# Adding epsilon by a reduction over (row sum, epsilon) pairs, with a newly set order of the work, in a fused attention and feed-forward kernel

## The chip, the cores and the metric

One core of one Trainium2 chip runs the whole program. The metric is device microseconds (us) of one execution of that core; lower is better. All data is float32.

## The reference

Block-causal attention over 8 batches of 8 heads (576 tokens, head width 64, blocks of 64), then two matrix products with a leaky ReLU between them on the 4608 x 512 result:

```python
scores = scale * np.matmul(q, k.transpose(0, 1, 3, 2))
scores = np.where(block_i >= block_j, scores, -1000000000.0)
scores = scores - np.max(scores, axis=-1, keepdims=True)
attn = np.exp(scores)
attn = attn / (np.sum(attn, axis=-1, keepdims=True) + 1e-09)
x = np.matmul(attn, v)            # heads side by side: 4608 x 512
h = x @ w_in                      # 512 x 2048
out = np.maximum(0.01 * h, h) @ w_out   # 2048 x 512
```

## The kernel before

Attention works head by head. The 576 query rows of a head are five tiles of up to 128 rows, tile t having 64, 192, 320, 448 or 576 keys. A head of the later batches goes through two softmax groups: tiles 3 and 2 (two rows of statistics, "128x2"), then tiles 4, 1 and 0 ("128x3"). The first batch is handled as 16 half heads. For each group `softmax` (line 502) plans: the score products on PE (TensorE) into the one PSUM pair `p_s` (L485 and L495); a mask and a negated row maximum `nm` on DVE (VectorE; L510 and L517); the exponential on ACT (ScalarE, L526), which also accumulates the row sums `sums`; then the pair of DVE instructions that the change is about, `sums + EPS` into `rec` (L541) and the reciprocal in place (L542); then `normalising` (line 548), which multiplies each row of probabilities `prow` by `rec` on POOL (GpSimd, L555), DVE (L556) or ACT (L557).

From the third batch on, the normalised rows are transposed in 32 x 32 pieces by DVE (`turn`, L733) and brought into place by a round trip through DRAM (`way`, `ptm`; L750 and L757, issued by SP). Every operand of a product is split into a high and a low float32r part: the high part is a cast (L244 on ACT, L245 on DVE), the low part a subtraction (L254 on DVE, L255 on POOL). So there are `pt` (probabilities), `vs`, `ks`, `qs` (L468), `xh`/`xl` (the feed-forward input) and `gh`/`gl` (the activated hidden layer).

The feed-forward layer takes the attention result in 18 chunks of 256 tokens. Each chunk has eight steps; a step is 24 products into `p_h` (L835), the activation `g` on ACT (L842), its split into `gh` and `gl`, and 12 products into `p_o` (L854). It runs behind the attention, and the two are interleaved on PE.

The order on every engine is set by a planner. Each piece of work is added with a rank, a cost in ns and the engines that could do it; `Plan.run` (line 104) walks through a time of its own and issues, on each free engine, the ready piece of lowest rank. The costs written in the program, the ranks' offsets (the table `RL` to `FILLTO`, lines 37 to 58) and the engine choices thus decide the order, which is then fixed in the program; on the chip every engine works through its list in order. A `DVE+` cost marks work that the planner doesn't put beside POOL work; L541 and L542 are marked plain `DVE` with 275 ns for both.

```python
def reciprocals():
    nc.vector.tensor_scalar_add(rec[z][:, a:e], sums[z][:, a:e], EPS)
    nc.vector.reciprocal(rec[z][:, a:e], rec[z][:, a:e])

add([("DVE", 275, reciprocals)], r, [("sum", z, at_col[t]) for t in ts], ...)
```

Of the kernel before, what the change touches and what calls it, by code (L numbers as in the profile page):

```python
# [9 lines left out]
F32 = mybir.dt.float32  # L10
# [3 lines left out]
ALU = mybir.AluOpType  # L14
AX = mybir.AxisListType
PSUM = bass.MemoryType.PSUM

P = 128
# [3 lines left out]
NT = 5  # L22
NEG = -1000000000.0
EPS = 1e-9
# [9 lines left out]
RAWS = 3  # L34
VALS = 3

RL = 1.277
RP = -34.119
RB = -28.274
RT = 2.311  # L40
RV = 3.081
RX = -25.651
RN = -61.868
RM = 0.934
RC = 15.092

LEAD = 2.356
LAG = 1.993
RS = 2.117
RG = 8.192  # L50
OFF1 = 4.961
SL1 = 10.108
AHEAD = -1.863

LAT = 1550
HOLD = 79.261
FILL = 235
FILLTO = -31.779


LOAD = 109
# [4 lines left out]
class Plan:  # L66
# [19 lines left out]
    def add(self, choices, rank, reads=(), writes=(), lag=0, kind=None):  # L86
        i = len(self.ops)
        deps = set()
        for k in reads:
            if k in self.writer:  # L90
                deps.add(self.writer[k])
        for k in writes:
            if k in self.writer:
                deps.add(self.writer[k])
            deps.update(self.readers.get(k, ()))
        for k in reads:
            self.readers.setdefault(k, []).append(i)
        for k in writes:
            self.writer[k] = i
            self.readers[k] = []  # L100
        deps.discard(i)
        self.ops.append((choices, rank, deps, lag, kind))

    def run(self):
# [15 lines left out]
        def offer(i):  # L120
            for k, choice in enumerate(self.ops[i][0]):
                e = choice[0]
                e = e[:3] if e == "DVE+" else e
                at = max([0] + [ends[d][1] + self.SYNC.get((ends[d][0], e), 0) for d in self.ops[i][2]])
                heapq.heappush(waiting, (at + k * HOLD, i, k))

# [101 lines left out]
def attention_ffn(ctx: ExitStack, tc: tile.TileContext, qk: bass.AP, v: bass.AP, w_in: bass.AP, w_out: bass.AP, out: bass.AP):  # L228
    nc = tc.nc
# [10 lines left out]
    add = plan.add  # L240
# [25 lines left out]
    def fixed(shape, dt, name, n=None, pool=const):  # L266
        if n is None:
            return pool.tile(shape, dt, name=name)
        return [pool.tile(shape, dt, name=f"{name}{i}") for i in range(n)]
# [20 lines left out]
    qn = [64, 128, 128, 128, 128]  # L290
# [13 lines left out]
    ks = fixed([P, 2, S], F32R, "ks", 2)  # L304
    kh, kl = ([ks[z][:, y] for z in range(2)] for y in range(2))
    vs = fixed([P, NT, 2 * D], F32R, "vs")
    nm = fixed([P, NT], F32, "nm", 2)
    sums = fixed([P, NT], F32, "sums", 2)
    rec = fixed([P, NT], F32, "rec", 2)
    for y in range(2):  # L310
        nc.gpsimd.memset(sums[y], 1.0)
    xr = [fixed([P, ND, S], F32, "xr0"), None]
    p_s = fixed([P, 2, 512], F32, "p_s", pool=psum)
    p_t = fixed([P, 512], F32, "p_t", 2, pool=psum)
# [40 lines left out]
    def weight_piece(num, rank, f, out_side, c0):  # L355
# [28 lines left out]
        if src.dtype != F32:  # L384
# [3 lines left out]

            add([("SP", 475, load)], rank - AHEAD, [], [r_key, t_key], lag=dma(w * P * 8))
            add(copying(w, val, top, by=2.0**-112), rank, [t_key], [v_key])  # L390
# [16 lines left out]
        else:  # L407
# [3 lines left out]

            add([("SP", 475, load)], rank - AHEAD, [], [v_key], lag=dma(w * P * 4))
        add(copying(w, lambda: hi, lambda: shaped(val())), rank, [v_key], [(key, 0)])
        add(subtracting(w, lambda: lo, lambda: shaped(val()), lambda: hi, "POOL"), rank, [v_key, (key, 0)], [(key, 1)])

    def attention(i):
        n, kind = work[i]
        b, h = divmod(n, H)
        z = i % 2
        r0 = float(i)  # L420
        y = z if b == 1 else 0
# [29 lines left out]

        add([("SP", {"full": 475, "lo": 650, "hi": 1300}[kind], load)], r0 - RL, [], [qkey], lag=dma((qe - qa + ke) * rows * 4))
        if plain_v:
            vt, vkey = lambda: vf[z][:, :nv], ("vf", z)
        else:
            vt, vkey = lambda: later["v_stage"][:, :nv], "vt"
        add([("SP", 475, lambda: nc.sync.dma_start(vt(), v[b, h, :, :nv]))], r0 - RL + 0.1, [], [vkey], lag=dma(nv * P * D * 4))
        rp = r0 - RP
        q_in, k_in = lambda: qkt()[:rows, 0, qa:qe], lambda: qkt()[:rows, 1, :ke]
# [40 lines left out]
        at_col = [(t - 2) % NT if kind == "full" else t for t in range(NT)]  # L500

        def softmax(tiles, mms, masks, r, both=None):
            banks = sorted({(sk, bk) for _, _, bk in tiles for bk in bk})
            add([("PE", list(scores(mms)))], r, qkd, banks)
            if both is not None:
                add([merging(*both, BLK)], r, [], banks)

            def mask():
                for ap in masks:
                    nc.vector.memset(ap, NEG)  # L510

            if masks:
                add([("DVE", sum(82 if len(ap.shape) == 2 else 140 for ap in masks), mask)], r, [], banks)
            for t, ap, bk in tiles:
                flat = len(ap.shape) == 2
                add(
                    [("DVE", dve(kw[t]), lambda t=t, ap=ap, flat=flat: nc.vector.tensor_reduce(  # L517
                        nm[z][: qn[t], at_col[t] : at_col[t] + 1], ap[: qn[t]], axis=AX.X if flat else AX.XY, op=ALU.max, negate=True
                    ))], r, [(sk, x) for x in bk], [("nm", z, at_col[t])],
                )  # L520

            def exponent(t, ap, flat):
                o = row(t, qn[t], pc[t], kw[t])
                if not flat:
                    o = o.rearrange("p (a k) -> p a k", a=2)
                nc.scalar.activation(  # L526
                    o, ap[: qn[t]], AF.Exp, bias=nm[z][: qn[t], at_col[t] : at_col[t] + 1], scale=1.0,
                    accum_out=sums[z][: qn[t], at_col[t] : at_col[t] + 1],
                )

            for t, ap, bk in tiles:
                add(
                    [("ACT", act(kw[t]) + 190, lambda t=t, ap=ap: exponent(t, ap, len(ap.shape) == 2))], r,
                    [("nm", z, at_col[tt]) for tt, _, _ in tiles] + [(sk, x) for x in bk], pkeys(t) + [("sum", z, at_col[t])],
                )

            ts = [t for t, _, _ in tiles]
            a, e = min(at_col[t] for t in ts), max(at_col[t] for t in ts) + 1

            def reciprocals():  # L540
                nc.vector.tensor_scalar_add(rec[z][:, a:e], sums[z][:, a:e], EPS)  # L541
                nc.vector.reciprocal(rec[z][:, a:e], rec[z][:, a:e])  # L542

            add([("DVE", 275, reciprocals)], r, [("sum", z, at_col[t]) for t in ts], [("rec", z, y) for y in range(a, e)])
            for t, _, _ in tiles:
                add(normalising(t, qn[t]), r - RN, [("rec", z, at_col[t])], pkeys(t))

# [24 lines left out]
        if kind != "lo":  # L572
# [3 lines left out]
            if kind == "full":  # L576
# [5 lines left out]
                masks = [pair(p_s[:BLK, 1, 224:480], 3)]  # L582
            softmax(tiles, mms, masks, r0 + RB, both)
        if flip:
            turn(i, row, pkeys)
        for base, c0, w, items in () if flip else tgroups[kind]:
            x = bank()
# [4 lines left out]

            add([("PE", [transpose(*y) for y in items])], r0 + RT, [k for t in sorted({a for a, _, _ in items}) for k in pkeys(t)] + ["ident"], [("t", x)])
            src = p_t[x][:, c0 : c0 + w]
            if plain_v:
                hi = ptf[:, base : base + w]
                add(copying(w, lambda hi=hi: hi, lambda src=src: src, sb=False), r0 + RT, [("t", x)], [("ptf", base)])
                continue
# [4 lines left out]
            def lo(base=base, w=w):  # L603
                return later["pt"][:, 1, base : base + w]

            add(copying(w, hi, lambda src=src: src, sb=False), r0 + RT, [("t", x)], [("pth", base)])
            add(
                subtracting(w, lo, lambda src=src: src, hi, sb=False)[:1],
                r0 + RT, [("t", x), ("pth", base)], [("ptl", base)],
            )  # L610
# [4 lines left out]
        vkey = ("vf", z) if plain_v else "vs"  # L615
        rv, rx = r0 + RV, r0 + RX

# [103 lines left out]
    def turn(i, row, pkeys):  # L721
# [6 lines left out]
        def flipped(t, s0, s1, step, j, r=0, n=P, k=1):  # L728
# [5 lines left out]

            add([("DVE", dve(k * P), go)], r0 + RT, pkeys(t), [("turn", t, j)])

# [11 lines left out]
        for b in range(4):  # L748
            add(
                [("SP", 475, lambda b=b: nc.sync.dma_start(way[z][b], later["turn"][:, b * w : (b + 1) * w]))],  # L750
                r0 + RM, ready, [("way", z, b)], lag=dma(P * w * 4),
            )
        for b in range(4):
# [4 lines left out]

            add([("SP", 475, back)], r0 + RM, [("way", z, b)], [("ptm", b)], lag=dma(P * w * 4))
        got = [("ptm", b) for b in range(4)]  # L760
        for a in range(4):
            hi = lambda a=a: later["pt"][:, 0, a * w : (a + 1) * w]
            lo = lambda a=a: later["pt"][:, 1, a * w : (a + 1) * w]
            raw = lambda a=a: later["ptm"][:, a * w : (a + 1) * w]
            add(copying(w, hi, raw), r0 + RC, got, [("pth", bases[a])])
            add(subtracting(w, lo, raw, hi), r0 + RC, got + [("pth", bases[a])], [("ptl", bases[a])])

# [56 lines left out]
    def ffn1(c, u, rank):  # L824
# [3 lines left out]
        for i in range(2):  # L828
# [11 lines left out]
            add([("PE", steps)], rank + i / 1000, ks + wkeys[("wi", f)], [("h", z)])  # L840
        rank += RG
        add([("ACT", act(512), lambda: nc.scalar.activation(g, hh, AF.Prelu, alpha=0.01))], rank, [("h", z)], ["g"])  # L842
# [33 lines left out]
    for num, (f, o, c) in enumerate(pieces):  # L876
        kind = "wo" if o else "wi"
        wkeys.setdefault((kind, f), []).extend([((kind, f, c), 0), ((kind, f, c), 1)])
        weight_piece(num, OFF1 + SL1 * (num + 1) / len(pieces), f, o, c)
    ready = []  # L880
# [5 lines left out]
    for i in range(len(work) + 1):  # L886
# [4 lines left out]
        if i in events:  # L891
# [3 lines left out]
            for k in range(num):  # L895
                c, u = here[k // NU], k % NU
                rank = i + LEAD + (nxt - i) * k / num
                if u == 0:
                    split_x(c, rank - RS)
                ffn1(c, u, rank)  # L900
# [41 lines left out]
```

## Time and profile before

| | us |
|---|---|
| median of 3 runs (1139.65 to 1141.52) | 1139.75 |
| the profiled execution | 1139.62 |
| its span, first to last instruction | 1137.9 |
| PE busy | 1082.0 (95%) |
| DVE busy | 856.8 (75%) |
| ACT busy | 686.9 (60%) |
| POOL busy | 484.0 (43%) |
| mean granted TensorE clock | 0.992 |

The program has stages with different limits: up to about 250 us the weights are loaded and split while the first batch is attended to; from 250 to about 970 us attention and feed-forward run side by side, less densely from 500 to 650 us; after that only the feed-forward layer is left. The shares of busy time over the whole span mix these stages, so the views are read by stretches. Busy PE time is a modelled figure, since products overlap.

### The profile page before, as it was taken

The page shows a single profiled execution, that of the slowest core. Times are in us where ns is not written, and L with a number is a line of the kernel's source. Part 1 is how long each engine was busy: PE and PEld are TensorE (multiplying, and loading weights), DVE is VectorE, ACT ScalarE, POOL GpSimd, SP SyncE. Part 2 cuts the span into 40 slices and gives each one's busy share as a digit, 9 for nine tenths or more (in the row PEclk, how much of TensorE's full clock was granted, in tenths as well). Part 3 has the DMA queues.
Part 4 walks back from the last instruction along what each step waited for, and adds up shares of the span by engine and source line. Part 5 has one row for each costly group of instructions (what it writes and reads, how often), then busy time and mean ns, then how long its engine had stood idle before and what let it go on. Part 6 is the DMA issues. An engine that isn't in the chain of part 4 may idle for free.

```text
span 1137.9 us, 20109 instructions
## 1 busy us (share of the span) xinstructions
PE 1082.0 (95%) x6792; PEld 961.0 (84%) x6792; DVE 856.8 (75%) x2047; ACT 686.9 (60%) x1637; POOL 484.0 (43%) x422
## 2 busy tenths in 40 slices
PE   6799999889998999899999999989999999999998
PEld 4577899778897988799999898879888898999997
DVE  6989888889899999967667699998999998400000
ACT  6888776768666666655555566666666766422222
POOL 2323454445544555433434445454544454322221
PEclk9999999989999999999999999999999999999999
DMA  6776331267665656454554565656666654300000
GB/s 201 226 215 219 115 102 54 86 185 227 202 180 161 197 163 188 150 166 128 157 153 129 164 182 164 186 163 176 177 199 175 180 164 147 84 19 10 11 19 19
DMA packets 94246, 166.20 MB, mean 146 GB/s; under 512 B 9664, under 2 KB 79296, under 8 KB 94144
## 3 DMA queue, kind: packets, MB, share of 16 engines
q1 hardware_dynamic: 94144, 164.93, 49.4%
q8 instruction: 53, 0.87, 0.4%
q14 instruction: 49, 0.40, 0.1%
HBM read 111.41 MB, written 53.48 MB: 145 GB/s over the span
## 4 chain that ended last, share of the span: by engine, by line
PE 53%; DVE 20%; ACT 8%; issue 7%; DMA 7%; POOL 3%; SPq 1%; DVEq 0%; POOLq 0%; ACTq 0%
PE p_h L835 22%; PE p_o L854 20%; PE p_s L495 4%; ACT prow L526 4%; DVE nm L517 4%; PE p_t L670 3%; DMA v_stage<-in_v 3%; DVE turn L733 2%; DVE rec L541 2%; DVE xl L254 2%; POOL gl L255 2%; DVE pt L254 2%; PE p_t L591 2%; POOL vs L255 1%; DMA out<-ob 1%
## 5 line engine op out<-in xcount | busy, mean ns | idle before, releaser
L835 PE MATMUL p_h<-xl,wih 128*128 128x256 f32 x1152 | 323.5, 281 | 9.1 <-DVE xl L254 9.1
L255 POOL TENSOR_TENSOR gl<-g,gh 128x512 fp32r<-128x512 f32 x131 | 177.0, 1351 | 355.4 <-ACT gh L244 218.7
L835 PE MATMUL p_h<-xh,wih 128*128 128x256 f32 x1152 | 326.1, 283 | 0.5 <-ACT xh L244 0.5
L835 PE MATMUL p_h<-xh,wil 128*128 128x256 f32 x1152 | 322.0, 279 | 0.0
L835 PEld LDWEIGHTS p_h<-xl,wih 128*128 128x128 f32 x1152 | 219.2, 190 | 21.1 <-DVE xl L254 11.6
L835 PEld LDWEIGHTS p_h<-xh,wih 128*128 128x128 f32 x1152 | 218.6, 190 | 10.3 <-ACT xh L244 0.7
L526 ACT ACTIVATE prow<-p_s,nm 128x576 f32<-128x576 f32 (+4 forms) x308 | 159.8, 526 | 101.4 <-DVE nm L517 100.6
L835 PEld LDWEIGHTS p_h<-xh,wil 128*128 128x128 f32 x1152 | 218.8, 190 | 0.0
L854 PE MATMUL p_o<-woh,gh 128*128 128x512 f32 x576 | 182.2, 398 | 0.0
L854 PE MATMUL p_o<-wol,gh 128*128 128x512 f32 x576 | 179.8, 394 | 0.0
L854 PE MATMUL p_o<-woh,gl 128*128 128x512 f32 x576 | 179.4, 393 | 0.0
L842 ACT ACTIVATE g<-p_h 128x512 f32<-128x512 f32 x144 | 85.1, 591 | 150.4 <-PE p_h L835 143.6
L255 POOL TENSOR_TENSOR pt<-ptm,pt 128x448 fp32r<-128x448 f32 x120 | 144.0, 1215 | 51.2 <-DVE pt L245 24.3
L557 ACT ACTIVATE prow<-prow,rec 128x320 f32<-128x320 f32 (+4 forms) x227 | 121.9, 571 | 71.6 <-DVE rec L542 68.7
L733 DVE STREAM_TRANSPOSE turn<-prow 128x384 f32<-128x384 f32 (+3 forms) x384 | 140.9, 397 | 18.5 <-ACT prow L557 6.2
L517 DVE TENSOR_REDUCE nm<-p_s 128x1 f32<-128x576 f32 (+4 forms) x308 | 137.8, 479 | 2.6
L854 PEld LDWEIGHTS p_o<-woh,gl 128*128 128x128 f32 x576 | 108.5, 188 | 24.1
L854 PEld LDWEIGHTS p_o<-wol,gh 128*128 128x128 f32 x576 | 108.9, 189 | 23.6
L495 PE MATMUL p_s<-ks,qs 128*128 128x288 f32 (+4 forms) x616 | 110.8, 314 | 19.0 <-ACT prow L526 18.4
L495 PEld LDWEIGHTS p_s<-ks,qs 128*128 128x128 f32 x616 | 89.5, 192 | 29.4 <-ACT prow L526 27.3
L670 PE MATMUL p_t<-pt,vs 128*128 128x512 f32 (+2 forms) x464 | 101.3, 348 | 1.1 <-DVE pt L254 1.0
L541 DVE TENSOR_SCALAR rec<-sums 128x3 f32<-128x3 f32 (+2 forms) x136 | 82.4, 606 | 24.5 <-ACT prow L526 19.9
(84 smaller groups left out, 1466.4 us busy)
## 6 DMA issues: line engine op xcount, KB each, us to landing
way<-turn SPq DMA_DIRECT2D x192, 224.0 KB, 2.3
ptm<-way SPq DMA_DIRECT2D x192, 224.0 KB, 4.3
qk_in<-in_qk SPq DMA_DIRECT2D x56, 576.0 KB, 4.8
v_stage<-in_v SPq DMA_DIRECT2D x56, 160.0 KB, 2.4
out<-ob SPq DMA_DIRECT2D x35, 256.0 KB, 2.4
raw<-in_w_in SPq DMA_DIRECT2D x16, 512.0 KB, 4.5
raw<-in_w_out SPq DMA_DIRECT2D x16, 512.0 KB, 4.3
qk_in<-in_qk SPq DMA_DIRECT2D x8, 320.0 KB, 3.7
```

What stands on the lines that cost most here:

```text
L254: ("DVE+" if sb else "DVE", dve(n), lambda: nc.vector.tensor_sub(dst(), one(), two())),
L255: ("POOL", pool2(n), lambda: nc.gpsimd.tensor_sub(dst(), one(), two())),
L495: go = lambda ap=ap, cols=cols, moving=moving, first=first, last=last: nc.tensor.matmul(ap, qs[z][:, cols], moving, start=first, stop=last)
L517: [("DVE", dve(kw[t]), lambda t=t, ap=ap, flat=flat: nc.vector.tensor_reduce(nm[z][: qn[t], at_col[t] : at_col[t] + 1], ap[: qn[t]], axis= ...
L526: nc.scalar.activation(o, ap[: qn[t]], AF.Exp, bias=nm[z][: qn[t], at_col[t] : at_col[t] + 1], scale=1.0, accum_out=sums[z][: qn[t], at_co ...
L541: nc.vector.tensor_scalar_add(rec[z][:, a:e], sums[z][:, a:e], EPS)
L557: ("ACT", act(kw[t], True), lambda: nc.scalar.mul(p(), p(), by)),
L670: nc.tensor.matmul(to, vs[:, j, :], src, start=start, stop=stop)
L733: nc.vector.transpose(dst, src.rearrange("p (s b i) -> p s b i", b=4, i=32))
L835: nc.tensor.matmul(hh[:, i, :], w[:, d, f * P : (f + 1) * P], x[:, d, :], start=k == 0, stop=k == len(terms) - 1)
L842: add([("ACT", act(512), lambda: nc.scalar.activation(g, hh, AF.Prelu, alpha=0.01))], rank, [("h", z)], ["g"])
L854: nc.tensor.matmul(p_o[m], a[:, i, m * P : (m + 1) * P], w[:, 2 * u + i, :], start=u == 0 and k == 0, stop=u == NU - 1 and k == 5,)
```

## The change

The row sums get a second column that holds epsilon, written once at the start by POOL. The scalar addition becomes a reduction over each (sum, epsilon) pair, on the same engine and in the same place before the reciprocal. The tiles of `nm` and `rec` become slices of one tile. The planner's cost of the pair goes from 275 to 290 ns, and 20 of its ordering constants get new values, of which two are shown.

```diff
-RG = 8.192
+RG = -1.11
...
-HOLD = 79.261
+HOLD = 64.646
...
-    nm = fixed([P, NT], F32, "nm", 2)
-    sums = fixed([P, NT], F32, "sums", 2)
-    rec = fixed([P, NT], F32, "rec", 2)
+    nmrec = fixed([P, 4, NT], F32, "nmrec")
+    nm, rec = ([nmrec[:, 2 * x + y] for y in range(2)] for x in range(2))
+    sums_of = fixed([P, 2, NT, 2], F32, "sums")
+    sums = [sums_of[:, y] for y in range(2)]
     for y in range(2):
         nc.gpsimd.memset(sums[y], 1.0)
+        nc.gpsimd.memset(sums[y][:, :, 1:2], EPS)
...
-                    accum_out=sums[z][: qn[t], at_col[t] : at_col[t] + 1],
+                    accum_out=sums[z][: qn[t], at_col[t], 0:1],
...
-                nc.vector.tensor_scalar_add(rec[z][:, a:e], sums[z][:, a:e], EPS)
+                nc.vector.tensor_reduce(rec[z][:, a:e], sums[z][:, a:e], axis=AX.X, op=ALU.add)
                 nc.vector.reciprocal(rec[z][:, a:e], rec[z][:, a:e])
 
-            add([("DVE", 275, reciprocals)], r, [("sum", z, at_col[t]) for t in ts], [("rec", z, y) for y in range(a, e)])
+            add([("DVE", 290, reciprocals)], r, [("sum", z, at_col[t]) for t in ts], [("rec", z, y) for y in range(a, e)])
```

Two lines are added above `softmax`, so L541 of before is L543 of the changed program, L556 is L558, L733 is L735.

How the order moves is shown at three places. The first is DVE, in a head of the third batch, around the second softmax group (tiles 4, 1, 0), before:

```order
L468 SCALAR_TENSOR_TENSOR qs_85<-qk_in_84,qs_85 64x576
L245 CAST gh_107<-g 128x512
L541 TENSOR_SCALAR rec_94<-sums_92 128x3
L542 RECIPROCAL rec_94<-rec_94 128x3
L556 TENSOR_SCALAR prow_1_72<-prow_1_72,rec_94 128x192
L556 TENSOR_SCALAR prow_0_71<-prow_0_71,rec_94 64x64
L733 STREAM_TRANSPOSE turn<-prow_1_72 128x2x4x32
```

The same place of DVE with the change:

```order
L470 SCALAR_TENSOR_TENSOR qs_85<-qk_in_84,qs_85 64x576
L245 CAST gh_105<-g 128x512
L254 TENSOR_TENSOR gl_107<-g,gh_105 128x512
L543 TENSOR_REDUCE nmrec<-sums 128x3
L544 RECIPROCAL nmrec<-nmrec 128x3
L558 TENSOR_SCALAR prow_4_75<-prow_4_75,nmrec 128x576
L735 STREAM_TRANSPOSE turn<-prow_1_72 128x2x4x32
```

One `gl` subtraction per head has come to DVE ahead of the pair, and DVE now normalises the row of 576 (ACT did) where it did those of 192 and 64 (ACT does).

The second is POOL's list for two heads of this kind, before:

```order
L255 TENSOR_TENSOR vs<-v_stage,vs 128x5x64
L255 TENSOR_TENSOR pt<-ptm,pt 128x448 x2
L255 TENSOR_TENSOR ks_87<-qk_in_84,ks_87 128x576
L255 TENSOR_TENSOR gl_109<-g,gh_107 128x512
L255 TENSOR_TENSOR gl_110<-g,gh_108 128x512
```

and with the change:

```order
L255 TENSOR_TENSOR vs<-v_stage,vs 128x5x64
L255 TENSOR_TENSOR pt<-ptm,pt 128x448 x2
L255 TENSOR_TENSOR ks_87<-qk_in_84,ks_87 128x576
L255 TENSOR_TENSOR gl_108<-g,gh_106 128x512
L255 TENSOR_TENSOR vs<-v_stage,vs 128x5x64
```

The `gl` of the step that DVE now does is gone from POOL; the other one has stayed.

The third is DVE where a new chunk's `xh` and `xl` are made, behind a second group, before:

```order
L733 STREAM_TRANSPOSE turn<-prow_4_75 64x4x32
L245 CAST xh<-xr_98 128x1024
L510 MEMSET p_s 64x2x64
L254 TENSOR_TENSOR xl<-xr_98,xh 128x1024
L261 TENSOR_REDUCE p_t_101<-p_t_101 128x128
L517 TENSOR_REDUCE nm_90<-p_s 128x1
```

and with the change:

```order
L735 STREAM_TRANSPOSE turn<-prow_4_75 64x4x32
L245 CAST xh<-xr_96 128x1024
L512 MEMSET p_s 64x2x64
L254 TENSOR_TENSOR xl<-xr_96,xh 128x1024
L261 TENSOR_REDUCE p_t_99<-p_t_99 128x128
L519 TENSOR_REDUCE nmrec<-p_s 128x1
```

Nothing has moved here.

## Rows read from the trace of the kernel before

**Rows 1.** Busy time by stretch: PE, PEld, DVE, ACT, POOL, granted clock, DMA share, GB/s
```profile
0.00:250.00 250.00, 223.75 (x1345) 185.90 (x1346) 211.81 (x525) 186.19 (x464) 96.33 (x102) 0.99 0.50 154
250.00:500.00 250.00, 238.81 (x1506) 214.39 (x1505) 229.61 (x545) 166.58 (x405) 125.31 (x105) 0.99 0.64 185
500.00:650.00 150.00, 149.30 (x964) 136.14 (x963) 103.07 (x256) 84.05 (x198) 61.20 (x55) 1.00 0.47 139
650.00:1000.00 350.00, 336.09 (x2112) 302.87 (x2111) 308.04 (x719) 216.97 (x517) 169.94 (x138) 0.99 0.58 167
```

**Rows 2.** Waits of PE from 250 to 1000 us: total us, times, longest
```profile
PE p_s L495 <- ACT prow L526: 16.4, 15, 2.9
PE p_h L835 <- DVE xl L254: 8.5, 7, 2.5
```

**Rows 3.** Busy time by stretch, the three 50 us stretches with a lowered clock
```profile
450.00:500.00 50.00, 46.98 (x295) 42.53 (x295) 43.22 (x104) 29.00 (x71) 21.18 (x18) 0.97 0.57 164
750.00:800.00 50.00, 45.67 (x282) 41.26 (x281) 44.71 (x104) 32.32 (x79) 23.97 (x20) 0.97 0.61 173
850.00:900.00 50.00, 47.49 (x293) 42.68 (x292) 46.35 (x110) 32.66 (x82) 24.94 (x22) 0.97 0.62 181
```

**Rows 4.** The timeline, 722 to 731 us: start, us, engine, instruction
```profile
721.80 0.43 DVE L245 CAST gh<-g 128x512 fp32r<-128x512 f32 x1
722.30 1.29 POOL L255 TENSOR_TENSOR gl<-g,gh 128x512 fp32r<-128x512 f32 x1 [2.34 <-PE p_o L854]
722.36 1.25 DVE L541 TENSOR_SCALAR rec<-sums 128x3 f32<-128x3 f32 x1
723.65 0.18 DVE L542 RECIPROCAL rec<-rec 128x3 f32<-128x3 f32 x1
...
729.29 1.15 POOL L255 TENSOR_TENSOR pt<-ptm,pt 128x448 fp32r<-128x448 f32 x1
729.68 0.78 DVE L541 TENSOR_SCALAR rec<-sums 128x2 f32<-128x2 f32 x1
730.50 0.17 DVE L542 RECIPROCAL rec<-rec 128x2 f32<-128x2 f32 x1
```

**Rows 5.** Groups of DVE by shape: count | busy us, mean ns | idle before
```profile
L541 DVE TENSOR_SCALAR rec<-sums 128x3 f32<-128x3 f32 x64 | 44.8, 700 | 10.2 <-ACT prow L526 6.5
...
L541 DVE TENSOR_SCALAR rec<-sums 128x2 f32<-128x2 f32 x56 | 35.3, 630 | 12.6 <-ACT prow L526 11.8
...
L542 DVE RECIPROCAL rec<-rec 128x3 f32<-128x3 f32 x64 | 11.4, 178 | 2.2
...
L541 DVE TENSOR_SCALAR rec<-sums 128x1 f32<-128x1 f32 x16 | 2.3, 146 | 1.8 <-ACT prow L526 1.6
```

**Rows 6.** Groups of DVE by shape, the other operations that are priced
```profile
L254 DVE TENSOR_TENSOR pt<-ptm,pt 128x448 fp32r<-128x448 f32 x72 | 61.4, 888 | 1.2 <-DMA qk_in<-in_qk 0.5 <-ACT pt L244 0.2
...
L517 DVE TENSOR_REDUCE nm<-p_s 64x1 f32<-64x64 f32 x60 | 12.1, 202 | 0.0
...
L254 DVE TENSOR_TENSOR gl<-g,gh 128x512 fp32r<-128x512 f32 x13 | 9.0, 696 | 3.6 <-ACT gh L244 3.4
...
L556 DVE TENSOR_SCALAR prow<-prow,rec 128x192 f32<-128x192 f32 x25 | 8.0, 321 | 0.9
...
L556 DVE TENSOR_SCALAR prow<-prow,rec 64x64 f32<-64x64 f32 x26 | 6.3, 240 | 0.0
...
L254 DVE TENSOR_TENSOR pt<-p_t,pt 128x448 fp32r<-128x448 f32 x8 | 4.9, 610 | 0.1
```

**Rows 7.** Line L541: duration min/median/max ns, and its busy time by stretch
```profile
L541 DVE TENSOR_SCALAR rec<-sums x136: 135/613/1273, 12.7 to 968.0; 128x3 f32<-128x3 f32 x64, 128x2 f32<-128x2 f32 x56, 128x1 f32<-128x1 f32 x16
...
250.00:500.00 250.00, 26.89 (x34) 0.99 0.64 185
...
650.00:1000.00 350.00, 38.87 (x42) 0.99 0.58 167
```

**Rows 8.** Chain of work that ended last, by line: 250 to 500, then 650 to 1000 us
```profile
by line: PE p_h L835 14.5%; issue 12.3%; PE p_o L854 11.0%; ACT prow L526 6.0%; DVE nm L517 4.9%; DMA v_stage<-in_v 4.8%; DMA ptm<-way 4.3%; PE p_s L495 3.8%; DVE turn L733 3.8%; DVE rec L541 3.6%; DMA out<-ob 3.5%; DVE xl L254 3.2%; POOL g
...
by line: PE p_h L835 18.3%; PE p_o L854 16.3%; issue 11.5%; ACT prow L526 5.9%; DMA v_stage<-in_v 5.7%; DVE nm L517 4.7%; PE p_s L495 4.0%; DVE rec L541 4.0%; POOL gl L255 3.7%; DVE turn L733 3.6%; PE p_t L670 3.2%; DVE xl L254 2.8%; POOL v
```

More of the change, by code (lines that the diff above doesn't have):

```diff
@@ L35 @@
 VALS = 3
[L37 to L47, printed above, removed]
-LAG = 1.993
-RS = 2.117
-RG = 8.192
-OFF1 = 4.961
-SL1 = 10.108
-AHEAD = -1.863
+RL = -5.006
+RP = -62.713
+RB = -2.888
+RT = 1.328
+RV = 3.024
+RX = 1.349
+RN = -43.93
+RM = -2.989
+RC = 10.678
+LEAD = 2.454
+LAG = 1.993
+RS = 3.401
+RG = -1.11
+OFF1 = 4.182
+SL1 = 11.846
+AHEAD = -2.179
 LAT = 1550
-HOLD = 79.261
+HOLD = 64.646
 FILL = 235
-FILLTO = -31.779
+FILLTO = -41.743
 LOAD = 109
```

## The prediction

> **What bounds the kernel now.** I read the busy time by stretch first. Between 250 and 1000 us, where attention and feed-forward run together, PE is busy for 724.2 of 750 us and DVE for 640.7 [rows 1]; leaving out 500 to 650 us, where attention is thin, DVE is busy for 537.6 of 600 us. So PE is the bound, and DVE is close enough behind it to make it wait: PE's idle time there is 25.8 us. The second view, PE's waits, says which waits these are: 16.4 us in 15 waits in which the scores could not be written because the exponential had not read `p_s` yet, and 8.5 us in 7 waits for `xl` [rows 2]. The exponential itself waits for the maximum, which DVE makes. [...]
>
> The third view is the timeline around the pair of instructions. L541 adds a constant to three numbers per row and takes 1.25 us: it starts 0.06 us after POOL has begun the subtraction `gl` and ends 0.02 us after POOL has (722.30 + 1.29 = 723.59 against 722.36 + 1.25 = 723.61). At 729.68 it again ends 0.02 us after POOL's `pt` does. The reciprocal behind it, on numbers of the same tile, takes 0.17 to 0.18 us [rows 4]. Over the run the 136 instructions at L541 take from 135 to 1273 ns, with a median of 613 [rows 7]: 82.4 us for what costs 135 ns when nothing is in the way. The shapes differ: three columns 700 ns, two 630, and one column 146 ns, 16 times [rows 5]. So the addition over two or three columns waits for whatever POOL is running, and the reciprocal does not. Last, the chain of work that ended last: L541 holds 3.6% of 250 us and 4.0% of 350 us there, 9.0 and 14.0 us, 23 us in all [rows 8].
>
> **The change, part by part.**
>
> *The addition becomes a reduction.* 136 TENSOR_SCALAR go, 82.4 us of DVE (44.8 + 35.3 + 2.3) [rows 5]. 136 TENSOR_REDUCE over two, four or six elements come. The trace has no such reduction from SBUF. Below, the bound is the unhindered addition of one column, 146 ns (19.9 us in all); above, nearest in kind, the shortest reduction from PSUM, 202 ns over 64 elements [rows 6], 27.5 us; far above, that it waits for POOL as the addition did, 82.4 us. I take 0.17 us, the reciprocal's price on the same tile (23 us), because it too is a tiny operation within SBUF, 64 + 56 times always short. DVE is freed of 59 us. Of L541's time, 26.9 + 38.9 us lie in the dense stretches, in 76 instructions [rows 7]; at 0.17 us each these would be 12.9 us, so 53 of the 59 us come free where DVE is busiest.
>
> [...]
>
> *The order.* Counted in the two programs, DVE gets 19 more `gl` (13 to 32), at 0.696 us [rows 6] 13.2 us. It normalised 25 rows of 192 and 26 of 64, 14.3 us; now it does 35 of 576, 7 of 448, 3 of 192, 8 of 64 and one of 320. From 64 to 192 columns the price rises by 81 ns, 0.63 ns a column [rows 6], so I estimate 0.56 us for 576 and 0.48 us for 448: 26 us, 12 us more. Other casts and subtractions that change engine cancel to within some 2 us. So 25 us of the 59 freed are given back as work, and 34 us stay free, still more than PE's 25.8 us of idle time. POOL loses the 19 `gl` and 19 of 42 normalisations; ACT gains 16 of them, at 60% busy. PE's order is the same at the places that I compared, and the `xh`-`xl` place does not move. No DMA is added, and the `memset` at the start is two more small POOL instructions beside the first loads.
>
> *What of it reaches the end.* The chain sets one limit. At 0.17 instead of up to 1.25 us, its pieces of L541, some 21 if each is about 1.1 us, would keep 3.6 of 23 us: at most 19.4 us. PE's idle time sets another: it cannot give back more than 25.8 us and 4.5 us of clock. Three terms, then. The score waits (16.4 us) are the end of DVE's queue: maximum, exponential, release of `p_s`. Where PE waits 1.1 us on average, DVE's list ahead is shorter by 1 us per head; I take three quarters, 12.3 us. The `xl` waits (8.5 us) start with PE itself, as `xh` cannot be overwritten before the last product of the chunk has read it, and the two instructions keep their place; only a late DVE goes away: a third, 2.8 us. Of the 4.5 us of clock, half, 2.2 us. The first 250 us hold 9.8 us of L541 in 45 pieces, but PE's 26 us of idle time there come with loads and the splitting of weights: nothing, give or take 5 us for the new order. From 1000 us on there is no L541. The sum is 12.3 + 2.8 + 2.2 = 17.3 us. The profiled execution takes 1139.62 us (span 1137.9 and 1.7 around it), 0.13 under the median: 1139.75 - 17.3 = 1122.5 us. Next in line is PE itself, which is why more than some 30 us cannot come out.
>
> **The rivals.**
>
> *The wait moves on.* Right behind the reciprocal now stands the normalisation of 576 columns, and `gl` right ahead; if POOL's work then falls beside these, they wait instead. For it: where the same 448-column subtraction reads SBUF on both sides it takes 888 ns, with one side in PSUM 610 [rows 6], so two-input work on DVE already waits 0.28 us on average. That on 32 `gl`, and the 0.53 us that the addition waited on average over three columns (0.70 - 0.17) on 35 normalisations, would take 9 + 18.6 of the 34 us that stayed free. Against it: the `gl` that ran on POOL at that moment is the very one that is taken away. A fifth of the waits would still go, some 3 to 5 us: 1135 to 1137 us; from nothing to 6 us, 1133 to 1142. [...]
>
> *The reduction waits as the addition did, or the extra work does not fit.* DVE then carries 25 us more in stretches where it is 90% busy, and PE waits at `p_s` more than before. It decides from the point where the reductions average over about 0.42 us (0.61 - 25/136). Between none and all of the 25 us would reach the end, as PE has feed-forward products to go on with; I take half: 12 us, 1152 us, range 1142 to 1158. Against it: the one-column addition and the reciprocal never wait [rows 5].
>
> *DVE was holding back all of it.* If every score wait and every fall of the clock goes and half the `xl` waits, 16.4 + 4.5 + 4.2 and up to 5 us at the start come out: 1110 us, and 1107 at the most.
>
> **How the numbers follow.** The forecast case, 10 to 28 us gained, 1112 to 1133 us, gets 0.62, since the rows show the wait, its cause and a PE that idles at DVE's hand. All of it (below 1112): 0.08. The wait moves on (1133 to 1142): 0.16, of which 0.06 lies below 1137.4. Slower, by DVE's extra work or by an order that is worse in the first 250 us: 0.14. A measurement of this kernel can tell 0.2%, 2.3 us. So faster 0.62 + 0.08 + 0.06 = 0.76, the same 0.10, slower 0.14. The range 1107 to 1142 us leaves out most of the slower case and little below.
>
> **What would show it.** The group at L543 (128x3, 128x2) should read 0.15 to 0.2 us with hardly a spread, 23 us in all, and L543 should be gone from the chain. DVE's busy time should fall by about 34 us, to 823 us. PE's score waits from 250 to 1000 us should fall from 16.4 to about 4 us. It would be wrong if L543 still ended with POOL's instructions; if L558 at 576 columns averaged over 1 us (the wait moved on); or if DVE's busy time fell and PE's waits stayed, which would mean that something other than DVE's queue sets when `p_s` comes free.

## The result, and the profile after

The changed kernel takes 1110.99 us (median of 4 runs, 1109.16 to 1112.38); the kernel before took 1140.28 us beside it (1139.65 to 1141.52). The ratio is 0.974, interval 0.972 to 0.976: faster. The forecast was 1122.5 us, in a range from 1107 to 1142. Every ratio below is against the kernel before, timed beside the run in question (1137.71 to 1140.28 us); of the four runs with all tiles 128 bytes further, one took 2718.75 us and is left out.

Busy time and the chain by engine, from the page of the kernel after:

```profile
span 1110.6 us, 20072 instructions
...
PE 1075.3 (97%) x6792; PEld 959.6 (86%) x6792; DVE 827.1 (74%) x2063; ACT 682.3 (61%) x1644; POOL 465.5 (42%) x401
...
PE 56%; DVE 24%; ACT 9%; issue 4%; DMA 4%; SPq 1%; POOL 0%; DVEq 0%; ACTq 0%
```

The span is 27.3 us shorter. PE's idle time over it fell from 1137.9 - 1082.0 = 55.9 to 35.3 us, by 20.6; its modelled busy time fell by 6.7 for the same 6792 products. POOL has left the chain (0%, 3% before). DVE's busy time fell by 29.7 us.

Busy time by stretch, after (columns as in [rows 1]), which answers to [rows 1]:

```profile
0.00:250.00 250.00, 227.05 (x1366) 189.73 (x1367) 214.05 (x547) 188.65 (x467) 96.07 (x103) 0.97 0.50 157
250.00:500.00 250.00, 244.01 (x1545) 220.65 (x1545) 226.07 (x560) 165.87 (x410) 119.17 (x98) 0.99 0.66 193
500.00:650.00 150.00, 149.73 (x968) 136.52 (x967) 97.74 (x251) 84.75 (x196) 75.44 (x63) 1.00 0.47 137
650.00:1000.00 350.00, 347.71 (x2237) 316.35 (x2237) 285.35 (x703) 216.61 (x529) 149.97 (x120) 1.00 0.56 162
```

The number in brackets behind PE's busy time counts products. From 650 to 1000 us PE does 2237 instead of 2112, from 250 to 500 us 1545 instead of 1506. At 350/2237 = 0.156 us each the 125 more are worth 19.6 us, the 39 some 6 us: the gain comes mostly from the two dense stretches, above all the second. The first 250 us give 21 products more, some 3 us. In them and the thin stretch between, PE's idle time fell from 25.8 to 8.6 us.

PE's waits from 250 to 1000 us, after, against [rows 2]:

```profile
PE p_s L497 <- ACT prow L528: 5.6, 8, 2.6
PE p_h L837 <- DVE xl L254: 2.7, 5, 0.6
```

Groups of DVE by shape, after, against [rows 5] and [rows 6]:

```profile
L254 DVE TENSOR_TENSOR pt<-ptm,pt 128x448 fp32r<-128x448 f32 x70 | 76.5, 1130 | 1.0 <-DMA way<-turn 0.3 <-ACT pt L244 0.3
L254 DVE TENSOR_TENSOR gl<-g,gh 128x512 fp32r<-128x512 f32 x32 | 23.0, 720 | 3.2 <-ACT gh L244 0.6
L558 DVE TENSOR_SCALAR prow<-prow,nmrec 128x576 f32<-128x576 f32 x35 | 18.2, 520 | 1.2
L543 DVE TENSOR_REDUCE nmrec<-sums 128x3 f32<-128x6 f32 x64 | 9.8, 152 | 6.7 <-ACT prow L528 5.6 <-ACT ptf L244 0.7
L543 DVE TENSOR_REDUCE nmrec<-sums 128x2 f32<-128x4 f32 x56 | 8.4, 149 | 2.8 <-ACT prow L528 2.0
L543 DVE TENSOR_REDUCE nmrec<-sums 128x1 f32<-128x2 f32 x16 | 2.3, 146 | 1.5 <-ACT prow L528 1.4
```

All reductions together (duration min/median/max ns):

```profile
L543 DVE TENSOR_REDUCE nmrec<-sums x136: 110/152/161, 12.9 to 940.4; 128x3 f32<-128x6 f32 x64, 128x2 f32<-128x4 f32 x56, 128x1 f32<-128x2 f32 x16
```

The reduction takes 152, 149 and 146 ns, whatever the number of columns, 20.5 us in all where the addition took 82.4. The subtraction `pt` has become slower (888 to 1130 ns). Counted over the trace before, 79 of the 120 additions over two and three columns start while POOL is at work; they take 0.93 us on average, and 76 of them end within 0.06 us of POOL's instruction. The other 41 take 0.17 us. Of the reductions after, 62 of 120 start while POOL is at work, and they take 0.15 us like the rest.

### The profile page after: what moved, and what is told of

It is laid out like the page before. It is cut to its first block, busy times and chain, and to the rows that moved or that the text cites. A ratio compares the mean times of both kernels' runs of the same rounds, so it can differ in the third digit from the quotient of the medians.

```text
span 1110.6 us, 20072 instructions
## 1 busy us (share of the span) xinstructions
PE 1075.3 (97%) x6792; PEld 959.6 (86%) x6792; DVE 827.1 (74%) x2063; ACT 682.3 (61%) x1644; POOL 465.5 (42%) x401
## 4 chain that ended last, share of the span: by engine, by line
PE 56%; DVE 24%; ACT 9%; issue 4%; DMA 4%; SPq 1%; POOL 0%; DVEq 0%; ACTq 0%
PE p_h L837 24%; PE p_o L856 21%; DVE turn L735 5%; DVE nmrec L519 4%; PE p_t L672 4%; PE p_s L497 4%; DVE pt L254 4%; ACT prow L528 3%; DVE qs L470 2%; ACT prow L559 2%; DMA raw<-in_w_in 2%; ACT pt L244 2%; PE p_t L593 2%; DVE gl L254 1%; DMA way<-turn 1%
## 5 line engine op out<-in xcount | busy, mean ns | idle before, releaser
L255 POOL TENSOR_TENSOR gl<-g,gh 128x512 fp32r<-128x512 f32 x112 | 155.9, 1392 | 422.0 <-ACT gh L244 387.7
L528 ACT ACTIVATE prow<-p_s,nmrec 128x576 f32<-128x576 f32 (+4 forms) x308 | 160.0, 526 | 71.4 <-DVE nmrec L519 70.0
L255 POOL TENSOR_TENSOR pt<-ptm,pt 128x448 fp32r<-128x448 f32 x122 | 148.3, 1228 | 37.1 <-DVE pt L245 19.2
L559 ACT ACTIVATE prow<-prow,nmrec 128x448 f32<-128x448 f32 (+4 forms) x243 | 118.3, 530 | 59.6 <-DVE nmrec L544 58.5
L735 DVE STREAM_TRANSPOSE turn<-prow 128x384 f32<-128x384 f32 (+3 forms) x384 | 142.3, 399 | 9.1 <-ACT prow L559 6.2
L519 DVE TENSOR_REDUCE nmrec<-p_s 128x1 f32<-128x576 f32 (+4 forms) x308 | 137.7, 479 | 2.6
L856 PEld LDWEIGHTS p_o<-woh,gh 128*128 128x128 f32 x576 | 92.4, 189 | 2.8 <-issue 0.4
```

The source lines that it names most:

```text
L255: ("POOL", pool2(n), lambda: nc.gpsimd.tensor_sub(dst(), one(), two())),
L528: nc.scalar.activation(o, ap[: qn[t]], AF.Exp, bias=nm[z][: qn[t], at_col[t] : at_col[t] + 1], scale=1.0, accum_out=sums[z][: qn[t], at_co ...
L559: ("ACT", act(kw[t], True), lambda: nc.scalar.mul(p(), p(), by)),
L735: nc.vector.transpose(dst, src.rearrange("p (s b i) -> p s b i", b=4, i=32))
L856: nc.tensor.matmul(p_o[m], a[:, i, m * P : (m + 1) * P], w[:, 2 * u + i, :], start=u == 0 and k == 0, stop=u == NU - 1 and k == 5,)
```

## The experiments

The first theory is that the operation alone makes the gain: the two- and three-column addition waits for POOL and the reduction does not. Its rival is that the new order makes it, above all the `gl` that no longer runs on POOL beside the pair. A third is that much of the gain is given back, since the wait moves to the next DVE instruction. After the first runs a fourth was formed, which the expectations call D: where the tiles behind `rec` lie in SBUF sets the pace of PE's products. The change keeps their places, since the merged tiles are together as long as the separate ones were; a straightforward edit does not.

### The operation alone

Old order, planner's cost left at 275, the reduction over pairs in separate tiles:

```diff
-    sums = fixed([P, NT], F32, "sums", 2)
+    sums = fixed([P, NT, 2], F32, "sums", 2)
...
+        nc.gpsimd.memset(sums[y][:, :, 1:2], EPS)
...
-                nc.vector.tensor_scalar_add(rec[z][:, a:e], sums[z][:, a:e], EPS)
+                nc.vector.tensor_reduce(rec[z][:, a:e], sums[z][:, a:e], axis=AX.X, op=ALU.add)
```

> The order of before (old constants, cost 275 kept), with only the addition made a reduction over pairs. Theory A (the operation carries the gain: the freed DVE is enough): the group reads 0.15 us, and 1118 to 1126 us, that is 15 to 22 of the 29 us. Rival B (the order carries it, the freed time is taken up by the next instruction that waits for POOL): 1134 to 1141 us, with longer DVE subtractions at L254 and L556. Rival C (the two only work together): 1127 to 1133 us.

Measured: 1121.40 us, ratio 0.984 [0.981, 0.986]. The reduction cost the same 158, 149 and 148 ns and PE's two waits fell to 1.1 and 1.9 us, yet the kernel is 10 us behind the changed one. This edit pushes every tile behind `rec` 64 bytes further. So it was run again with the merged tiles of the change, which leave those places as they were:

```diff
-    nm = fixed([P, NT], F32, "nm", 2)
-    sums = fixed([P, NT], F32, "sums", 2)
-    rec = fixed([P, NT], F32, "rec", 2)
+    nmrec = fixed([P, 4, NT], F32, "nmrec")
+    nm, rec = ([nmrec[:, 2 * x + y] for y in range(2)] for x in range(2))
+    sums_of = fixed([P, 2, NT, 2], F32, "sums")
+    sums = [sums_of[:, y] for y in range(2)]
...
```

> The order of before with the reduction, and the tiles of nm, rec and sums merged as in the change, so that all tiles behind them (xr0, gh, gl, xh, xl, pt and on) keep the addresses of before; in the run with the reduction in the old order they lay 64 bytes further, and its feed-forward products followed each other every 120 ns instead of 114 even where nothing else ran. Theory D (the place of the tiles slows the products, some 17 to 20 us in all): 1100 to 1107 us, products of p_h every 114 ns. Rival E (the place does nothing, the run without the addition was faster for its lack of 136 instructions): 1118 to 1123 us.

Measured: 1109.64 us, ratio 0.975 [0.974, 0.977], as much as the whole change gives (and 2.6 us above the range that D expected). The old order lets one compare place by place. The timeline of this kernel at the pair that [rows 4] show (the 104th; columns as there):

```profile
705.18 1.31 POOL L255 TENSOR_TENSOR gl<-g,gh 128x512 fp32r<-128x512 f32 x1 [1.25 <-DVE gh L245]
...
705.23 0.16 DVE L543 TENSOR_REDUCE nmrec<-sums 128x3 f32<-128x6 f32 x1
705.43 0.18 DVE L544 RECIPROCAL nmrec<-nmrec 128x3 f32<-128x3 f32 x1
705.64 1.12 DVE L558 TENSOR_SCALAR prow<-prow,nmrec 128x192 f32<-128x192 f32 x2
...
705.70 0.78 ACT L559 ACTIVATE prow<-prow,nmrec 128x576 f32<-128x576 f32 x1 [0.50 <-DVE nmrec L544]
```

POOL has begun `gl` 0.05 us earlier, as before, and runs it for 1.31 us, but the reduction is through in 0.16 us. Of the two normalisations behind it (1.12 us together) the first, of 192 columns, now lasts 0.96 us, until 0.11 us after POOL is done: the wait has moved on, past what ACT needs here. ACT waited 0.50 us for `rec` here; in the kernel before it waited 1.59 us, with the activation `g` queued behind, as its timeline shows:

```profile
723.92 0.78 ACT L557 ACTIVATE prow<-prow,rec 128x576 f32<-128x576 f32 x1 [1.59 <-DVE rec L542]
724.61 0.57 ACT L842 ACTIVATE g<-p_h 128x512 f32<-128x512 f32 x1
725.21 0.62 ACT L244 CAST gh<-g 128x512 fp32r<-128x512 f32 x1
```

Waits of ACT from 250 to 1000 us (total us, times, longest), before:

```profile
ACT prow L526 <- DVE nm L517: 84.7, 81, 2.6
ACT prow L557 <- DVE rec L542: 59.2, 71, 1.6
ACT g L842 <- PE p_h L835: 53.9, 36, 4.8
```

and with the reduction in the old order:

```profile
ACT g L844 <- PE p_h L837: 119.4, 75, 4.8
ACT prow L528 <- DVE nmrec L519: 56.9, 77, 2.2
...
ACT prow L559 <- DVE nmrec L544: 25.5, 44, 1.3
```

and of the changed kernel:

```profile
ACT g L844 <- PE p_h L837: 97.0, 68, 4.3
ACT prow L528 <- DVE nmrec L519: 55.8, 74, 3.3
ACT prow L559 <- DVE nmrec L544: 47.7, 50, 2.5
```

In the old order the wait for `rec` more than halves, but in the changed kernel it falls only to 47.7 us, and both take the same time, so this wait does not set it. What falls alike in both is the wait of the exponential for the row maximum, 84.7 to 56.9 and 55.8 us: the path that the prediction named. And `g` waits for PE's products 75 and 68 instead of 36 times: ACT is ready for them earlier. What DVE gives back with the reduction in the old order, in that kernel's groups by shape, against [rows 6]:

```profile
L254 DVE TENSOR_TENSOR pt<-ptm,pt 128x448 fp32r<-128x448 f32 x72 | 76.1, 1092 | 1.4 <-ACT pt L244 0.8
L558 DVE TENSOR_SCALAR prow<-prow,nmrec 128x192 f32<-128x192 f32 x25 | 23.2, 928 | 0.9
```

The 192-column normalisation goes from 321 to 928 ns, `pt` from 888 to 1092: 15 us each. DVE is freed of 82.4 - 20.8 = 61.6 us, and its busy time falls by only 36 us (to 820.7), but the gain is there.

### The order alone

The changed kernel with the scalar addition, and separate sums, back:

```diff
...
-                nc.vector.tensor_reduce(rec[z][:, a:e], sums[z][:, a:e], axis=AX.X, op=ALU.add)
+                nc.vector.tensor_scalar_add(rec[z][:, a:e], sums[z][:, a:e], EPS)
```

> The order of the changed program (new constants, cost 290), with the old addition of a scalar to separate sums. Theory A: the addition waits for POOL again, 0.4 to 0.6 us on average, and DVE carries some 25 us of moved work besides: 1132 to 1150 us. Rival B: 1111 to 1122 us. Rival C: 1127 to 1140 us.

Measured: 1136.09 us, ratio 0.998 [0.997, 0.999]. Here the later tiles lie 32 bytes nearer; the second run has 32 unused bytes in front of them, `fixed([P, 8], F32, "pad")`, so that all lie as before:

> The order of the change with the scalar addition, and an unused tile of 32 bytes that puts all tiles behind at the addresses of before. Theory D: p_h products every 114 ns instead of 118, and 1118 to 1130 us. Rival E: as without the pad, 1134 to 1139 us.

Measured: 1131.74 us, ratio 0.994 [0.992, 0.996], between the two ranges expected. The order by itself is worth 7 us. Its additions among the groups of DVE:

```profile
L542 DVE TENSOR_SCALAR nmrec<-sums 128x2 f32<-128x2 f32 x56 | 37.3, 665 | 2.4 <-ACT prow L527 1.6
...
L542 DVE TENSOR_SCALAR nmrec<-sums 128x3 f32<-128x3 f32 x64 | 21.0, 328 | 7.3 <-ACT prow L527 6.1 <-ACT ptf L244 0.7
```

and its PE's waits from 250 to 1000 us:

```profile
PE p_s L496 <- ACT prow L527: 15.4, 15, 2.4
PE p_h L836 <- DVE xl L254: 3.9, 6, 1.0
```

The new order, which takes that `gl` off POOL, halves the three-column addition (700 to 328 ns), not the two-column one (630 to 665), and PE's score waits stay (16.4 to 15.4 us). With the reduction nothing is left for the order to save: old order 0.975 [0.974, 0.977], new order 0.974 [0.972, 0.976].

### Another way to add, and no addition

Is it the reduction, or any other form than TENSOR_SCALAR? The sum was made as a two-input addition from a tile of epsilons, in the old order:

```diff
+    eps = fixed([P, NT], F32, "eps")
+    nc.gpsimd.memset(eps, EPS)
...
-                nc.vector.tensor_scalar_add(rec[z][:, a:e], sums[z][:, a:e], EPS)
+                nc.vector.tensor_add(rec[z][:, a:e], sums[z][:, a:e], eps[:, a:e])
```

> The order of before; the addition is a TENSOR_TENSOR of two SBUF tiles (sums and a tile of epsilon). If what waits is an instruction that reads SBUF twice at once beside POOL, this one waits as well: 0.5 to 0.7 us on average, ending with POOL's instructions, and 1136 to 1143 us. Rival: only the scalar form is slow beside POOL: 0.15 to 0.2 us, and the time of the reduction in the same order.

```profile
L543 DVE TENSOR_TENSOR rec<-sums,eps 128x3 f32<-128x3 f32 x64 | 44.3, 692 | 10.6 <-ACT prow L528 6.8
L543 DVE TENSOR_TENSOR rec<-sums,eps 128x2 f32<-128x2 f32 x56 | 35.0, 626 | 12.6 <-ACT prow L528 11.8
...
L543 DVE TENSOR_TENSOR rec<-sums,eps 128x1 f32<-128x1 f32 x16 | 3.9, 243 | 1.5 <-ACT prow L528 1.5
```

Measured: 1143.58 us, ratio 1.005 [1.003, 1.006]. It waits like the scalar addition (692 and 626 ns against 700 and 630), so the gain is a property of the form. (Its tile moves later ones by 32 bytes, and in the tail products into `p_h` start every 117 instead of 114 ns; part of the half per cent may be that.) Form and width together decide: of the 16 additions over one column three start while POOL is at work, and there the scalar form takes 145 to 155 ns, the two-input form 559 to 801; the reduction of the changed kernel takes at most 161 anywhere. What in the chip sets the forms apart is not shown by these runs.

Then the addition was left out, first in the old order:

```diff
-                nc.vector.tensor_scalar_add(rec[z][:, a:e], sums[z][:, a:e], EPS)
-                nc.vector.reciprocal(rec[z][:, a:e], rec[z][:, a:e])
+                nc.vector.reciprocal(rec[z][:, a:e], sums[z][:, a:e])
```

> The order of before; the addition of epsilon is left out, the reciprocal reads the sums. Theory A: 136 times 0.15 us less on DVE than with the reduction, 20 us, of which a third to a half reaches the end: 7 to 10 us faster than the reduction in the same order, 1109 to 1118 us. Rival B: 1130 to 1140 us. If it is within 2 us of the reduction in the old order, DVE has stopped being what PE waits for.

Measured: 1101.61 us, ratio 0.967 [0.965, 0.969], below the 1109 us that was the least expected; the same in the new order:

> The order of the change, addresses as before, the addition of epsilon left out. If the new order suits the freed DVE better than the old one, 1085 to 1100 us, below the 1101.6 us of the old order without the addition. If its extra work on DVE (gl, the rows of 576) only costs, 1103 to 1110 us.

Measured: 1102.68 us, ratio 0.969 [0.967, 0.970], between the two ranges expected. Again the orders do not differ. PE's waits from 250 to 1000 us, old order, are nearly gone:

```profile
PE p_h L834 <- DVE xl L254: 0.7, 1, 0.7
PE p_s L495 <- ACT prow L526: 0.3, 1, 0.3
```

and among its groups of DVE the normalisation of 192 columns has taken the wait with POOL over (321 ns before):

```profile
L555 DVE TENSOR_SCALAR prow<-prow,rec 128x192 f32<-128x192 f32 x25 | 27.9, 1115 | 0.9
```

So the some 20 us that the reductions still cost are worth, by the ratios, 9 us in the old order and 6 in the new, and the 61.6 us between addition and reduction 29: some 0.3 to 0.5 us of the kernel for each us of DVE ahead of the normalisation. This version beats both kernels. A row sum holds the exponential of its own maximum, so it is at least 1, and adding 1e-9 to such a float32 changes nothing.

### The places of the tiles

The kernel before with 64 unused bytes a partition behind `rec`:

```diff
     rec = fixed([P, NT], F32, "rec", 2)
+    fixed([P, 16], F32, "pad")
```

> The kernel before with an unused tile of 64 bytes per partition behind rec, nothing else. Theory D: p_h products every 120 ns where nothing else runs; where DVE was the limit part of it is covered, so 1143 to 1160 us. Rival E: 1136 to 1142 us, 114 ns.

Measured: 1146.61 us, ratio 1.007 [1.006, 1.009]: the shift alone costs 8 us. Which tile's place counts? The kernel without the addition got the 64 bytes ahead of `xh` only:

> The kernel without the addition (1101.6 us, order of before), with an unused tile of 64 bytes a partition ahead of xh: xh, xl, the output tiles and the transposed probabilities lie 64 bytes further, while gh, gl and the first input tile keep their place. Theory (the place of the product's operand xh or xl counts): products into p_h follow each other every 120 ns in the tail where only the feed-forward layer is left, and the time is 1108 to 1120 us. Rival (it is the place of gh, gl or of other tiles): 114 ns and 1100 to 1104 us.

Measured: 1114.05 us, ratio 0.979 [0.977, 0.980], against 0.967 unshifted. And 128 bytes behind `rec`:

> The kernel without the addition (1101.6 us, order of before), with an unused tile of 128 bytes a partition behind rec, so that every later tile lies 128 bytes further. Theory (what counts is the place within 128 bytes, as the shift of 64 slowed and this one restores it): 114 ns between products into p_h in the tail, 1100 to 1104 us. Rival (any shift away from the places of before slows): about 120 ns and 1108 to 1120 us.

Measured: 1114.6 us, ratio 0.980 [0.978, 0.981]: the theory of a period of 128 bytes falls. The chain from 1000 to 1090 us, where only the feed-forward layer is left (start us, us, what), unshifted:

```profile
1008.08 1.39 PE p_h L834 x12
1009.46 1.37 PE p_o L853 x6
```

with `xh` and what lies behind it 64 bytes further:

```profile
1002.65 1.44 PE p_h L835 x12
1004.09 1.39 PE p_o L854 x6
```

and with all 128 bytes further:

```profile
1001.14 1.41 PE p_h L835 x12
1002.55 1.40 PE p_o L854 x6
```

Twelve products into `p_h` take 1.44 instead of 1.39 us (median distance of two starts 120 instead of 114 ns). There are 288 such dozens and as many sixes of `p_o`, 0.02 us longer: 14 and 6 us if all of them followed each other closely; the time grew by 12.4 us. Since `gh`, `gl` and the first input tile kept their places here, what counts for `p_h` is the place of `xh` or `xl`, or of a tile behind them. It is not only the operand's own place: `p_o` reads `gh`, `gl` and weights, none of which moved here, and its six still took 1.39 instead of 1.37 us. With all tiles 128 bytes further two starts into `p_h` are 118 ns apart, and `p_o` at 0.03 us more per six loses more than with 64. Which rule of the address stands behind this is open; it was not tried further.

## Why the prediction was right, and where it fell short

The mechanism held, and the time lies in the range; the gain is 28.8 us against the 1139.75 us that the sum went by, where the sum had 17.3.

- **The reduction's price.** Taken at 0.17 us and 23 us in all; measured 0.15 us and 20.5 us, at most 161 ns with POOL's work beside it. The bound at 82.4 us, that it waits too, is out.
- **DVE's busy time.** Forecast 823 us, measured 827.1. The work given back by the order was close to its 25 us: 14.0 us more for `gl`, 14.5 more for the normalisation (35 rows of 576 columns at 0.52 us, estimated 0.56). The total is near in part by luck: `pt` took 15.1 us more, which the sum did not hold, and the remaining groups some 11 us less, where it let them cancel.
- **PE's idle time.** Score and `xl` waits were to give back 12.3 + 2.8 = 15.1 us. Measured: 16.4 to 5.6 and 8.5 to 2.7, together 16.6 us, and PE's idle time between 250 and 1000 us 17.2. The two together were sized nearly right; the scores gave 10.8 rather than 12.3, `xl` 5.8 rather than 2.8.
- **The step that fell short** is the pair of limits, "The chain sets one limit" (at most 19.4 us) and "PE's idle time sets another" (25.8 and 4.5 us), with the sum kept to fractions of the second. The change gained 28.8 us, so what the chain held of L541 was no cap. The second limit was passed by the kernel without the addition, 36 us faster. The span fell by 27.3 us, of which 17.2 are idle time between 250 and 1000 us, 3.3 idle time in the first 250 us (26.25 to 22.95), where the sum had nothing, and 6.7 PE's busy time, where it had 2.2 for the clock. That busy time is modelled: in the tail a product is shown for 276 ns, and the next starts 114 ns later, so a delay of up to 162 ns, by this estimate, would show as no idle at all. PE's busy time fell further, to 1069.9 us, without the addition (old order), for the same 6792 products. That such hidden delays are what went is inferred, not shown.
- **The clock** does not explain it. The sum's 2.2 us for it is half of 4.5 us, by an estimate from [rows 3]: 3% of 50 us in each of three stretches. No run shows that such time comes back; what they show in its place is the granted clock. The three falls of [rows 3] are gone (1.00 in all three stretches of the kernel after), but earlier ones have deepened; busy time by stretch of the kernel after (PE busy, granted clock, DMA share, GB/s):

```profile
200.00:250.00 50.00, 44.58 (x254) 0.86 0.45 135
250.00:300.00 50.00, 47.24 (x285) 0.93 0.68 203
450.00:500.00 50.00, 48.98 (x316) 1.00 0.64 193
```

  and of the kernel before:

```profile
200.00:250.00 50.00, 43.87 (x262) 0.93 0.42 127
250.00:300.00 50.00, 48.15 (x301) 1.00 0.73 209
```

  By the same estimate, 7% of 50 us, the clock costs 3.5 us more in each of these two stretches, against the 4.5 of the three falls: the 2.2 us counted for it did not come from there.
- **What was left out** is ACT's list. The prediction followed DVE to the maximum and the exponential; that ACT stood 59.2 us waiting for `rec` between 250 and 1000 us, with `g` and `gh` behind it, was not in it. But little hangs on it: that wait is 25.5 us with the reduction in the old order and 47.7 in the changed kernel, for the same time of the kernel, while the wait for the maximum fell by 28 and 29 us.
- **The rivals.** "The wait moves on" happened: the 192-column normalisation (old order) and `pt` took waits over. It did not undo the gain, though `pt` is not off the path: it holds 4% of the chain of the changed kernel, 2% before. "The reduction waits as the addition did, or the extra work does not fit" fell with the 0.15 us. "DVE was holding back all of it" came nearest in time, 1110 us, by another route: not all of PE's waits went. This case, below 1112 us, had a chance of 0.08, and the forecast case, 1112 to 1133 us, had 0.62; so the time lies in the range only because the range reached down to this rival. (A gain of 10 to 28 us, as the forecast case is also put, ends at 1130 us, not at 1133.) The order, which the prediction counted as 25 us of DVE lost, is worth nothing measurable beside the reduction.

## What to carry to other kernels

A tiny instruction on DVE that lasts as long as whatever POOL runs beside it (here 0.93 us on average, and 0.17 us without POOL) is worth replacing by a form that does not wait (here 0.15 us), or by nothing; judge it by who is queued behind it (here above all the next row maximum on DVE, for which the exponential and then PE wait), and expect the wait to reappear at a later instruction of a form that waits (here 321 to 928 ns for the normalisation of 192 columns, in the old order); here that did not undo the gain. A chain of waits shows one path, and modelled busy time can hide short stalls (here of up to 162 ns, by the estimate above), so here neither the chain nor PE's idle time capped the gain. When an edit changes a tile's size, compare at equal places of all other tiles: here 64 bytes were worth 8 to 12 us.

## What the runs showed that was not expected

- The pace of PE's products depends on where tiles lie in SBUF, and not on the operands' own place alone: 114, 118 or 120 ns between products into `p_h` for shifts of 0, 128 and 64 bytes, with 1101.6, 1114.6 and 1114.1 us for the kernel without the addition (the 64 bytes ahead of `xh`).
- Of three ways to add epsilon to three columns, the scalar form took 700 ns, the two-input form 692 ns and the reduction over pairs 157 ns, in the same order of the work, though the reduction reads six elements a row, like the two-input form.
